# Two attention-fed feed-forward layers on one core: two border operands read out of PSUM, a slack in the planner, a shorter stretch of attention, and hidden values of the second part kept in PSUM

## The chip, the core and the metric

The kernel runs on one core of a Trainium2 chip, as one program. The metric is the device time of one execution in microseconds (us), lower is better. The core has a matrix engine (PE, with its weight loads PEld), a vector engine (DVE), a scalar engine (ACT), a second, general vector engine (POOL) and SP, which here only issues DMA transfers. Each works through its own instructions strictly in the order in which they were written; semaphores order them against each other. SBUF is the on-chip memory. PSUM is the small memory that PE writes to, here eight banks of 128 x 512 floats. GpSimd (POOL) is given no PSUM operand anywhere in this kernel.

## The reference

```python
def reference(q, k, v, w_gate, w_val, w_out1, w_in, w_out2):      # names shortened
    x = attention(q, k, v)                # 4 x 8 heads x 576 x 64, causal window of 128, ALiBi bias, softmax
    x = x.transpose(0, 2, 1, 3).reshape(2304, 512)
    g = x @ w_gate                        # 512 x 1536
    x = (g * sigmoid(g) * (x @ w_val)) @ w_out1       # 1536 x 512
    h = x @ w_in                          # 512 x 2048
    return (h * sigmoid(h)) @ w_out2      # 2048 x 512, all in float32
```

## The kernel before

The 2304 tokens are worked on in three **parts** of 768 (six tiles of 128). For each part come attention, the first feed-forward layer (`moe1`, six groups of 256 hidden columns) and the second (`moe2`, eight groups). The attention of a part is spread over the feed-forward work of the part before it, so that PE has something in all gaps. In the trace the second part's layers lie from about 375 to 680 us, with the third part's attention spread over them.

A float32 product is made of three passes of rounded pieces: each operand is split into `hi` (a rounded copy) and `lo` (the rest), so every operand costs a copy and a subtraction. The copy is `copy_op` (ACT, or DVE instead; line 348 or 349). The subtraction is `sum_op`: with `psum=True` always DVE (line 357), else POOL (line 358) or DVE, whichever the planner finds free earlier.

Each group's input products go by Strassen's scheme: `quad` runs seven products into three PSUM banks X, Y, Z with small sums in between. The second of them goes to bank Y; then DVE adds a saved product to Y in place (`add_to`, line 948), ACT copies Y out (`copy`, line 348), and only then may the fifth product overwrite Y. Between them PE has two other products (12 matmuls). `L963` is the last sum of `quad`, into a `tmp` buffer. The Strassen operands of the tokens are seven slots of the tile `XOP`. They are made at the **borders** between two layers by `operands`, out of `ACC` (the sums of `moe1`'s output) or `XST` (attention output, or `moe2`'s input side): some slots are split directly, the others are differences that `less` (line 693) writes into PSUM first. Slot 0 holds the first block (tokens 0 to 383 of the part) and feeds the first product of the next layer.

After `quad`, `hidden1` or `hidden2` apply the activation (`tanh`, line 1015, and `times`, line 1026). With `psum=False` the last `times` writes an SBUF buffer `tmp`, which frees the PSUM bank, and the split reads `tmp`. With `psum=True` it writes back into the PSUM bank, and the split into `h` reads the bank and frees it. One of the four blocks of a group has no bank, and goes by `tmp` in either case. Part one and the last groups of part three run with True, part two with False.

`out1` (lines 1182 to 1196) and `out2` (lines 1212 to 1227) multiply `h` by the output weights `wo` (three buffers) and add into `ACC`. In part two, `out_sums` also makes Strassen sums of output weights for part three: it fetches two halves of a weight (`word` and `top`, line 865), adds them, forms four `sums`, splits each into a `later_raw` buffer and stores that to DRAM (line 769).

The order on every engine comes from a **planner**: each operation is handed to `plan.add` with an estimated cost, a due time, what it reads and writes, and the banks it takes or gives. `issue` then plays a clock: per engine it takes the ready operation of the earliest due time and writes it down. An operation's estimated ready time is

```python
ready_at[m][o] = max(ready_at[m][o], end + handover(o, e))
```

where `handover` is what the planner counts from one engine's end to another's start, in ns (the first name is the one that waits):

```python
HANDOVER = {
    "pe": {"act": 370, "dve": 360, "pool": 300},
    "act": {"pe": 200, "dve": 128, "pool": 85},
    "dve": {"pe": 200, "act": 145, "pool": 85},
```

The clock is only an estimate. What it writes is the fixed order in which the engine will run, so an operation that is really later than planned holds up all that stands behind it.

Of the kernel before, what the change touches and what calls it, by code (L numbers as in the profile page):

```python
# [20 lines left out]
P = 128  # L21
# [35 lines left out]
class Plan:  # L57
# [18 lines left out]

    def add(self, engine, cost, due, fn, reads=(), writes=(), take=None, give=None, port=False, other=()):
        n = len(self.ops)
        preds = set()
        for key in reads:  # L80
            if key in self.writer:
                preds.add(self.writer[key])
            self.readers.setdefault(key, []).append(n)
        for key in writes:
            if key in self.writer:
                preds.add(self.writer[key])
            preds.update(self.readers.pop(key, ()))
            self.writer[key] = n
        preds.discard(n)
        if isinstance(take, Bank):  # L90
            take = (take,)
        ways = {e: (c, f, p or e == "pool", d) for e, c, f, p, d in [(engine, cost, fn, port, 0.0), *other]}
        self.ops.append((ways, due, preds, take, give))

    def issue(self):
# [25 lines left out]
        def start(e, n, now):  # L121
            ways, _, _, take, _ = ops[n]
            if ways[e][2]:
                now = max(now, port_free)
            if take is not None:
                m = len(take)
                if len(self.banks) < m or any(used[k] + m > self.limits[k] for k in kinds(take[0])):
                    return None
                now = max(now, heapq.nsmallest(m, self.banks)[-1][0])
            if len(ways) > 1 and min(ways, key=lambda o: done(o, n)) != e:  # L130
                return None
            return now
# [27 lines left out]
        while left:  # L160
# [5 lines left out]
            s, n = best  # L166
            ways, due, _, take, give = ops[n]
            cost, fn, port, _ = ways[e]
# [24 lines left out]
            for m in succs[n]:  # L193
                for o in ready_at[m]:
                    ready_at[m][o] = max(ready_at[m][o], end + handover(o, e))
                missing[m] -= 1
                if not missing[m]:
                    offer(m)
# [3 lines left out]
def attention_moe_moe2_kernel(  # L202
# [46 lines left out]
    GP = 3  # L249
# [96 lines left out]

    def copy_op(n, due, out, src, reads, writes, give=None, psum=True):
        act = lambda: nc.scalar.activation(out(), src(), AF.Copy)  # L348
        dve = lambda: nc.vector.tensor_copy(out(), src())
        plan.add(  # L350
            "act", cost("act_ps" if psum else "act", n), due, act, reads, writes, give=give,
            other=[("dve", cost("dve", n), dve, not psum, 500.0)],
        )

    def sum_op(n, due, out, x, y, op, reads, writes, give=None, psum=False):

# [4 lines left out]
        else:  # L361
            plan.add(
                "pool", cost("pool", n), due, pool, reads, writes, give=give,
                other=[("dve", cost("dve", n), dve, True, 500.0)],
            )
# [308 lines left out]
    def operands(src, name, due, plain=True):  # L674
# [5 lines left out]
        def block(j, blk, kk):  # L680
            c = 2 * j + kk
            return (
                lambda: src[:, blk * BT:blk * BT + BT, c, :],
# [18 lines left out]
        for kk in range(2):  # L702
            t1[kk] = less(b[0, 1, kk], b[0, 0, kk])
            t2[kk] = less(b[1, 1, kk], t1[kk])
# [56 lines left out]

    def split_weight(dst, key, src, reads, n, due, old=()):
        out = dst if callable(dst) else lambda: dst
        copy_op(n, due, lambda: out()[:, 0], lambda: src, reads, [key, *old], psum=False)
        sum_op(n, due, lambda: out()[:, 1], lambda: src, lambda: out()[:, 0].bitcast(F32), ALU.subtract, reads, [key])

# [20 lines left out]

    def strassen_sums(a, due):
        def add(x, y, op):
            i = take("sum", len(SUM_R))  # L790
            t, tk = SUM_R[i], ("sum", i)
            (xa, xk), (ya, yk) = x, y
            sum_op(2 * P, due, lambda: t, lambda: xa, lambda: ya, op, xk + yk, [tk])
            return t, [tk]
# [61 lines left out]
    def out_sums(kind, g, due, behind):  # L856

        a = {}
        for j in range(2):
# [9 lines left out]
            for i in range(2):  # L869
                a[i, j] = (w[:, 2 * P * i:2 * P * i + 2 * P], [wk])  # L870
        for n, (t, tk) in enumerate(strassen_sums(a, due)):
            m = take("stage", len(STAGE))
            u, uk = STAGE[m][0], ("stage", m)
            split_weight(u, uk, t, tk, 2 * P, due, before.pop(uk, ()))
            store(KEPT["s" + kind][g, n], lambda u=u: flat(u()), uk, ("kept", "s" + kind, g, n), due, 730.0)
# [289 lines left out]
    def value2(c, due):  # L1165
# [5 lines left out]
        return value  # L1171

    def out1(g, ws, d, blk, hs, due):
        b0, nb = blk
# [17 lines left out]
        keys = [("acc", b0 + t, d) for t in range(nb)]  # L1192
        if g == 0:
            copy_op(n, due, lambda: acc, pv, [b], keys, give=b)
# [34 lines left out]

    WLEAD = 19050.0  # L1230
    pend = []
    jobs = [("1", g) for g in range(G1 - 1)] + [("2", g) for g in range(G2 - 2)]
# [137 lines left out]
    operands(XST, "xt", state["t"])  # L1370
    spread(2, state["t"] + 6000.0, M1 + M2 - 8000.0)
    moe1(1, range(GP), "sum", False)
    moe1(1, range(GP, G1), "kept", False)
    flush()
    operands(ACC, "acc", state["t"])
    moe2(1, "kept", False)
    flush()
# [41 lines left out]
```

## Time and profile before

| | us |
|---|---|
| three timed executions | 935.42, 941.37, 941.68 (median 941.37) |
| the profiled execution | 937.67, of which the span from first to last instruction is 936.0 |
| PE busy in the span | 907.9 |
| DVE, POOL, ACT busy in the span | 708.9, 559.6, 531.0 |

A line such as `L948 DVE TENSOR_TENSOR bank<-bank,tmp` is one group of instructions: line of the kernel, engine, operation, what it writes and reads. "Idle before" is time that the engine stood still ahead of them and `<-` what ended it.

### The profile page before, as it was taken

Reading aid. Unit: us, or ns where it says so; the run is one execution under the profiler, and the core shown is the slowest. Engines: PE = TensorE matmul, PEld = TensorE weight load, DVE = VectorE, ACT = ScalarE, POOL = GpSimd, SP = SyncE. Lnnn points to the kernel's source line nnn. Section 1 sums busy time; section 2 is a strip of 40 time slices with the busy share of each in tenths; the row PEclk is TensorE's granted clock in tenths of the full one; section 3 lists DMA queues with packets and bytes.
Section 4 is the critical chain, followed back from the end, with each engine's and each line's share of the span. In section 5 each row is a group of like instructions: output and inputs, shape, how many; then the busy total and the mean of one; then the engine's idle time right before and its main releaser. Section 6 shows DMA issues by size and latency. Waiting matters only on the chain.

```text
span 936.0 us, 17803 instructions
## 1 busy us (share of the span) xinstructions
PE 907.9 (97%) x5758; PEld 843.8 (90%) x5758; DVE 708.9 (76%) x1602; ACT 531.0 (57%) x1361; POOL 559.6 (60%) x635
## 2 busy tenths in 40 slices
PE   7999999998999999999999999999999999999998
PEld 5799999997888888989999988888799999999996
DVE  7888879879889788647565867667755776778875
ACT  6887567757877675664343575445355333474431
POOL 2865468777657678785524487754144445876453
PEclk9999999999999999999999999999999999999999
DMA  9988997996897987999877789988498888678702
GB/s 222 281 243 258 283 324 221 294 313 206 274 304 260 305 290 265 354 314 304 279 219 244 242 292 330 312 284 311 151 329 249 251 253 253 201 234 245 218 23 91
DMA packets 181677, 241.58 MB, mean 258 GB/s; under 512 B 68048, under 2 KB 97232, under 8 KB 181584
## 3 DMA queue, kind: packets, MB, share of 16 engines
q1 hardware_dynamic: 181584, 240.44, 80.0%
q8 instruction: 46, 0.75, 0.3%
q14 instruction: 47, 0.39, 0.1%
HBM read 169.61 MB, written 70.78 MB: 257 GB/s over the span
## 4 chain that ended last, share of the span: by engine, by line
PE 69%; DVE 12%; DMA 7%; POOL 4%; ACT 4%; issue 3%; SPq 0%; DVEq 0%; POOLq 0%; ACTq 0%
PE bank L902 13%; PE bank L904 12%; PE bank L903 12%; PE bank L1212 4%; PE bank L1214 4%; PE bank L1213 4%; PE bank L607 3%; PE bank L493 3%; PE bank L1182 2%; PE bank L1184 2%; PE bank L1183 2%; DVE word L755 2%; DMA top<-kept_o 2%; PE bank L1118 1%; PE bank L1120 1%
## 5 line engine op out<-in xcount | busy, mean ns | idle before, releaser
L902 PE MATMUL bank<-XOP,wu 128*128 128x384 f32 (+1 forms) x868 | 297.3, 343 | 11.6 <-DVE tmp L963 4.3
L903 PE MATMUL bank<-XOP,wu 128*128 128x384 f32 (+1 forms) x868 | 288.9, 333 | 2.5 <-POOL XOP L358 1.9
L904 PE MATMUL bank<-XOP,wu 128*128 128x384 f32 (+1 forms) x868 | 288.9, 333 | 0.0
L902 PEld LDWEIGHTS bank<-XOP,wu 128*128 128x128 f32 x868 | 163.1, 188 | 23.0 <-ACT tmp L348 8.2
L903 PEld LDWEIGHTS bank<-XOP,wu 128*128 128x128 f32 x868 | 163.3, 188 | 4.4 <-POOL XOP L358 2.1
L904 PEld LDWEIGHTS bank<-XOP,wu 128*128 128x128 f32 x868 | 163.0, 188 | 0.1
L358 POOL TENSOR_TENSOR h<-tmp,h 128x384 fp32r<-128x384 f32 x77 | 81.7, 1071 | 62.0 <-ACT h L348 60.9
L348 ACT ACTIVATE tmp<-bank 128x384 f32<-128x384 f32 x133 | 62.1, 488 | 52.8 <-PE bank L904 28.2
L1026 DVE SCALAR_TENSOR_TENSOR tmp<-tmp,bank 128x384 f32<-128x384 f32 (+1 forms) x120 | 64.4, 542 | 36.4 <-ACT tmp L1015 24.4
L1212 PE MATMUL bank<-wo,h 128*128 128x512 f32 (+1 forms) x218 | 87.3, 401 | 1.7 <-DMA wo<-kept_o 1.7
L1214 PE MATMUL bank<-wo,h 128*128 128x512 f32 (+1 forms) x218 | 85.6, 393 | 0.0
L1213 PE MATMUL bank<-wo,h 128*128 128x512 f32 (+1 forms) x218 | 85.6, 393 | 0.0
L553 POOL TENSOR_TENSOR cs<-cs,st 128x512 f32<-128x512 f32 x36 | 39.9, 1109 | 65.8 <-DVE st L550 44.7
L1224 DVE TENSOR_TENSOR ACC<-bank,ACC 128x512 f32<-128x512 f32 (+1 forms) x97 | 64.1, 678 | 15.4 <-PE bank L1214 14.6
L358 POOL TENSOR_TENSOR wu<-word,wu 128x256 fp32r<-128x256 f32 x63 | 51.1, 824 | 39.4 <-ACT wu L348 35.2
L348 ACT ACTIVATE h<-tmp 128x384 fp32r<-128x384 f32 x97 | 49.5, 523 | 41.9 <-PE bank L1213 20.0
L1182 PE MATMUL bank<-h,wo 128*128 128x384 f32 (+1 forms) x216 | 72.5, 336 | 0.1
L1183 PE MATMUL bank<-h,wo 128*128 128x384 f32 (+1 forms) x216 | 71.5, 331 | 0.1
L1184 PE MATMUL bank<-h,wo 128*128 128x384 f32 (+1 forms) x216 | 71.4, 330 | 0.0
L1015 ACT ACTIVATE tmp<-bank 128x384 f32<-128x384 f32 (+1 forms) x121 | 57.0, 482 | 25.0 <-PE bank L904 11.5
L755 DVE SCALAR_TENSOR_TENSOR word<-raw,top 128x512 int32<-128x512 int32 x68 | 60.9, 895 | 11.7 <-ACT top L752 9.6
L948 DVE TENSOR_TENSOR bank<-bank,tmp 128x384 f32<-128x384 f32 x93 | 52.1, 561 | 22.1 <-PE bank L904 20.3
(414 smaller groups left out, 2149.6 us busy)
## 6 DMA issues: line engine op xcount, KB each, us to landing
wu<-kept_i SPq DMA_DIRECT2D x112, 256.0 KB, 3.5
wu<-kept_g SPq DMA_DIRECT2D x72, 256.0 KB, 4.2
wu<-kept_v SPq DMA_DIRECT2D x72, 256.0 KB, 4.3
wo<-kept_o SPq DMA_DIRECT2D x34, 512.0 KB, 4.7
raw<-in_moe_w_out_dram SPq DMA_DIRECT2D x28, 512.0 KB, 4.9
kept_o<-wo SPq DMA_DIRECT2D x28, 512.0 KB, 4.4
kept_i<-wu SPq DMA_DIRECT2D x56, 256.0 KB, 4.5
kept_s<-later_raw SPq DMA_DIRECT2D x44, 256.0 KB, 4.8
```

Of the source, the lines that this page charges most:

```text
L348: act = lambda: nc.scalar.activation(out(), src(), AF.Copy)
L358: pool = lambda: nc.gpsimd.tensor_tensor(out(), x(), y(), op)
L755: lambda: nc.vector.scalar_tensor_tensor(w.bitcast(I32), word, 13, top, ALU.logical_shift_right, ALU.bitwise_or),
L902: nc.tensor.matmul(ps, wh, xh, start=start, stop=False, skip_group_check=True)
L903: nc.tensor.matmul(ps, wh, xl, start=False, stop=False, skip_group_check=True)
L904: nc.tensor.matmul(ps, wl, xh, start=False, stop=stop, skip_group_check=True)
L1182: nc.tensor.matmul(ps[:, 0:n], wh, h[:, 0], start=(i == 0), stop=False)
L1183: nc.tensor.matmul(ps[:, 0:n], wh, h[:, 1], start=False, stop=False)
L1184: nc.tensor.matmul(ps[:, 0:n], wl, h[:, 0], start=False, stop=(i == 1))
L1212: nc.tensor.matmul(ps, hh, wh, start=(i == 0), stop=False)
L1213: nc.tensor.matmul(ps, hh, wl, start=False, stop=False)
L1214: nc.tensor.matmul(ps, hl, wh, start=False, stop=(i == 1))
```

## The change

1. `plan.add` gets a `slack`, which is added to the estimated ready time. `strassen_sums` and the splits inside `out_sums` get 4000 ns of it; the addition of the two fetched halves ahead of them doesn't.
2. At the border from `moe1` to `moe2`, in all three parts, the last group's sums for the first block's first two column blocks stay in PSUM: the sum is written over the bank, and `operands` makes slot 0 and the first difference from there.
3. The attention of the third part is spread over a stretch that is 20,000 planner ns shorter.
4. Part two runs `moe1` and `moe2` with `psum=True`.

```diff
-    def add(self, engine, cost, due, fn, reads=(), writes=(), take=None, give=None, port=False, other=()):
+    def add(self, engine, cost, due, fn, reads=(), writes=(), take=None, give=None, port=False, other=(), slack=0.0):
...
-                    ready_at[m][o] = max(ready_at[m][o], end + handover(o, e))
+                    ready_at[m][o] = max(ready_at[m][o], end + handover(o, e) + ops[m][5])
...
         def block(j, blk, kk):
             c = 2 * j + kk
+            if src is ACC and j == 0 and blk == 0:
+                return (lambda b=left[kk]: tiles(b.tile[:, 0:N])), [left[kk]]
...
-            t1[kk] = less(b[0, 1, kk], b[0, 0, kk])
+            held = src is ACC
+            t1[kk] = less(b[0, 1, kk], b[0, 0, kk], x_keys(0, kk) if held else (), left[kk] if held else None)
...
-        for n, (t, tk) in enumerate(strassen_sums(a, due)):
+        for n, (t, tk) in enumerate(strassen_sums(a, due, LATE)):
             m = take("stage", len(STAGE))
             u, uk = STAGE[m][0], ("stage", m)
-            split_weight(u, uk, t, tk, 2 * P, due, before.pop(uk, ()))
+            split_weight(u, uk, t, tk, 2 * P, due, before.pop(uk, ()), LATE)
...
-        if g == 0:
+        if g == G1 - 1 and b0 == 0 and d < 2:
+            plan.add("dve", cost("dve", n), due, lambda: nc.vector.tensor_tensor(pv(), pv(), acc, ALU.add), keys, [b])
+            left[d] = b
+        elif g == 0:
...
+    LATE = 4000.0
...
-    spread(2, state["t"] + 6000.0, M1 + M2 - 8000.0)
-    moe1(1, range(GP), "sum", False)
-    moe1(1, range(GP, G1), "kept", False)
+    spread(2, state["t"] + 6000.0, M1 + M2 - 28000.0)
+    moe1(1, range(GP), "sum", True)
+    moe1(1, range(GP, G1), "kept", True)
...
-    moe2(1, "kept", False)
+    moe2(1, "kept", True)
```

What it does to the order shows at three places. First DVE at the border from `moe1` to `moe2` of the first part (215 to 221 us of the trace before). `bank_132` and `bank_134` are the last output sums of the first block, lines 1196 and 693 of before are 1205 and 695 of after, and the sum that stays in PSUM is line 1200. Before:

```order
L1196 TENSOR_TENSOR ACC<-bank_132,ACC 128x3x128
L357 TENSOR_TENSOR XOP<-bank_129,XOP 128x384
L1196 TENSOR_TENSOR ACC<-bank_134,ACC 128x3x128
L1196 TENSOR_TENSOR ACC<-bank_135,ACC 128x3x128
L1196 TENSOR_TENSOR ACC<-bank_133,ACC 128x3x128
L693 TENSOR_TENSOR bank_130<-ACC 128x384
L693 TENSOR_TENSOR bank_132<-ACC,bank_130 128x384
```

After:

```order
L1200 TENSOR_TENSOR bank_132<-bank_132,ACC 128x384
L357 TENSOR_TENSOR XOP<-bank_129,XOP 128x384
L1200 TENSOR_TENSOR bank_134<-bank_134,ACC 128x384
L357 TENSOR_TENSOR XOP<-bank_132,XOP 128x384
L695 TENSOR_TENSOR bank_130<-ACC,bank_132 128x384
L357 TENSOR_TENSOR XOP<-bank_134,XOP 128x384
L695 TENSOR_TENSOR bank_132<-ACC,bank_130 128x384
L758 SCALAR_TENSOR_TENSOR word_98<-raw_94,top_95 128x512
L1205 TENSOR_TENSOR ACC<-bank_135,ACC 128x3x128
```

The two `lo` halves of slot 0 (`XOP<-bank_132`, `XOP<-bank_134`) now stand on DVE right behind the sums that they need; before, they stood on POOL, behind weights. A weight operation (`word_98`) has moved up into the border, ahead of the remaining sums.

Second, ACT in the third group of the second part (around 417 us before). `later_raw` are the splits of `out_sums`, `qts` and `KR` belong to attention, and line 1015 (1018 after) is the tanh. Before:

```order
L348 ACTIVATE KR<-bank_129 128x2x128
L348 ACTIVATE later_raw_256_4727<-sums 128x256
L1015 ACTIVATE tmp_108<-bank_134 128x384
L348 ACTIVATE later_raw_256_4727<-sums 128x256
L456 ACTIVATE qts<-bank_131 128x256
L348 ACTIVATE later_raw_256_4746<-sums 128x256
L1015 ACTIVATE tmp_110<-tmp_111 128x384
L348 ACTIVATE later_raw_256_4746<-sums 128x256
```

After:

```order
L348 ACTIVATE KR<-bank_132 128x2x128
L348 ACTIVATE tmp_109<-bank_129 128x384
L348 ACTIVATE tmp_110<-bank_128 128x384
L456 ACTIVATE qts<-bank_133 128x256
L1018 ACTIVATE tmp_108<-bank_130 128x384
L348 ACTIVATE later_raw_256_4773<-sums 128x256
L1018 ACTIVATE tmp_110<-tmp_111 128x384
L1018 ACTIVATE tmp_109<-bank_128 128x384
L1018 ACTIVATE tmp_111<-bank_129 128x384
L348 ACTIVATE later_raw_256_4825<-sums 128x256
```

The first split of `out_sums` has moved behind the first tanh and behind two copies of `quad`, and only two of the four stand in this stretch.

Third, SP at the end of the second part (around 665 us before). `wo_91<-kept_o_142` is the second half of the output weights of the last group, `kept_s` are the stores of `out_sums`, `later_l` are weights of the third part in buffers that attention used. Before:

```order
L772 DMA wu_79<-kept_g 128x512
L891 DMA later_l_256_7182<-kept_o_141 128x2x256
L891 DMA later_l_256_7185<-kept_o_141 128x2x256
L772 DMA wo_91<-kept_o_142 128x1024
L891 DMA later_u_256_7200<-kept_s_143 128x512
```

After:

```order
L775 DMA wu_79<-kept_g 128x512
L772 DMA kept_s_144<-later_raw_256_4825 128x512 x2
L775 DMA wo_91<-kept_o_142 128x1024
L775 DMA wo_92<-kept_o_141 128x1024
L772 DMA kept_s_144<-later_raw_256_4773 128x512
```

The fetch into `wo_91` no longer stands behind `later_l`, but behind two stores of `out_sums`, whose data POOL makes behind six operations on `XST` for the next border.

## Rows read from the trace of the kernel before

**Rows 1.** Page, busy time, share of the span and instructions of each engine.

```profile
PE   907.9 (97%) x5758; PEld 843.8 (90%) x5758; DVE 708.9 (76%) x1602; ACT 531.0 (57%) x1361; POOL 559.6 (60%) x635
```

**Rows 2.** Page, the chain that ended last, by engine.

```profile
PE 69%; DVE 12%; DMA 7%; POOL 4%; ACT 4%; issue 3%; SPq 0%; DVEq 0%; POOLq 0%; ACTq 0%
```

**Rows 3.** Waits of PE, 200 to 240 us: total us, times, longest us.

```profile
PE bank L903 <- POOL XOP L358: 1.9, 1, 1.9
PE bank L902 <- ACT tmp L348: 1.9, 2, 1.1
PE bank L902 <- DVE tmp L349: 0.7, 1, 0.7
```

**Rows 4.** Waits of PE, 240 to 375 us.

```profile
PE bank L902 <- DVE tmp L963: 1.9, 3, 1.2
PE bank L902 <- DVE tmp L349: 1.0, 1, 1.0
```

**Rows 5.** Waits of PE, 375 to 680 us.

```profile
PE bank L902 <- DVE tmp L963: 2.4, 3, 1.9
PE bank L902 <- ACT tmp L348: 2.2, 4, 0.8
PE bank L1212 <- DMA wo<-kept_o: 1.7, 1, 1.7
PE bank L903 <- DVE XOP L357: 0.2, 1, 0.2
```

**Rows 6.** Waits of PE, 680 to 936 us.

```profile
PE bank L1120 <- DVE later_cs L357: 0.6, 1, 0.6
PE bank L902 <- DVE bank L693: 0.3, 1, 0.3
```

**Rows 7.** Windows: us, busy us of PE, PEld, DVE, ACT, POOL; clock, DMA.

```profile
240.00:375.00 135.00, 132.04 (x762) 114.05 (x761) 117.28 (x247) 95.78 (x244) 93.53 (x112) 1.00 0.84 282
375.00:680.00 305.00, 298.35 (x1833) 275.11 (x1832) 205.17 (x466) 155.24 (x405) 175.61 (x207) 1.00 0.84 280
```

**Rows 8.** Timeline of PE, 203 to 232 us: start, us, what, idle before.

```profile
220.16 0.45 PE L903 MATMUL bank<-XOP,wu 128*128 128x384 f32 x1 [1.87 <-POOL XOP L358]
...
229.11 0.34 PE L903 MATMUL bank<-XOP,wu 128*128 128x384 f32 x1
229.28 0.34 PE L904 MATMUL bank<-XOP,wu 128*128 128x384 f32 x1
```

**Rows 9.** Timeline of POOL, 203 to 232 us.

```profile
216.53 1.31 POOL L358 TENSOR_TENSOR wo<-word,wo 128x512 fp32r<-128x512 f32 x1
217.80 6.52 POOL L358 TENSOR_TENSOR XOP<-ACC,XOP 128x384 fp32r<-128x384 f32 x6
```

**Rows 10.** Timeline of ACT, 414 to 420 us.

```profile
417.60 0.42 ACT L348 ACTIVATE later_raw<-sums 128x256 fp32r<-128x256 f32 x1 [2.11 <-POOL sums L358]
417.92 0.47 ACT L1015 ACTIVATE tmp<-bank 128x384 f32<-128x384 f32 x1
```

**Rows 11.** Timeline of POOL, 404 to 422 us.

```profile
415.46 1.30 POOL L358 TENSOR_TENSOR word<-word,top 128x512 f32<-128x512 f32 x1 [2.05 <-DMA word<-kept_o]
```

**Rows 12.** Groups of instructions by form, 375 to 680 us.

```profile
L358 POOL TENSOR_TENSOR h<-tmp,h 128x384 fp32r<-128x384 f32 x39 | 40.8, 1057 | 28.4 <-ACT h L348 28.4
L348 ACT ACTIVATE tmp<-bank 128x384 f32<-128x384 f32 x58 | 27.1, 488 | 22.6 <-PE bank L904 11.3 <-DVE bank L948 11.0
L948 DVE TENSOR_TENSOR bank<-bank,tmp 128x384 f32<-128x384 f32 x40 | 22.3, 561 | 11.3 <-PE bank L904 10.3 <-ACT tmp L348 0.8
L348 ACT ACTIVATE later_raw<-sums 128x256 fp32r<-128x256 f32 x44 | 18.0, 414 | 30.7 <-POOL sums L358 26.0 <-DMA kept_s<-later_raw 4.2 <-ACT tmp L348 0.5
L357 DVE TENSOR_TENSOR h<-tmp,h 128x384 fp32r<-128x384 f32 x17 | 11.6, 697 | 2.3 <-ACT h L348 1.9
```

**Rows 13.** Groups of instructions by form, whole span.

```profile
L357 DVE TENSOR_TENSOR h<-bank,h 128x384 fp32r<-128x384 f32 x50 | 27.5, 550 | 5.3 <-ACT h L348 4.6
```

**Rows 14.** Timeline of SP, 640 to 684 us.

```profile
665.52 0.33 SPq L772 DMA_DIRECT2D wo<-kept_o  x1
```

More of the change, by code (lines that the diff above doesn't have):

```diff
@@ L92, in add @@
         ways = {e: (c, f, p or e == "pool", d) for e, c, f, p, d in [(engine, cost, fn, port, 0.0), *other]}
-        self.ops.append((ways, due, preds, take, give))
+        self.ops.append((ways, due, preds, take, give, slack))
     def issue(self):
@@ L121, in start @@
         def start(e, n, now):
-            ways, _, _, take, _ = ops[n]
+            ways, _, _, take, _, _ = ops[n]
             if ways[e][2]:
@@ L166, in issue @@
             s, n = best
-            ways, due, _, take, give = ops[n]
+            ways, due, _, take, give, _ = ops[n]
             cost, fn, port, _ = ways[e]
@@ L345, in cost, with copy_op @@
         return a + b * n
-    def copy_op(n, due, out, src, reads, writes, give=None, psum=True):
+    def copy_op(n, due, out, src, reads, writes, give=None, psum=True, slack=0.0):
         act = lambda: nc.scalar.activation(out(), src(), AF.Copy)
@@ L351, in copy_op, with sum_op @@
             "act", cost("act_ps" if psum else "act", n), due, act, reads, writes, give=give,
-            other=[("dve", cost("dve", n), dve, not psum, 500.0)],
+            other=[("dve", cost("dve", n), dve, not psum, 500.0)], slack=slack,
         )
-    def sum_op(n, due, out, x, y, op, reads, writes, give=None, psum=False):
+    def sum_op(n, due, out, x, y, op, reads, writes, give=None, psum=False, slack=0.0):
         dve = lambda: nc.vector.tensor_tensor(out(), x(), y(), op)
@@ L363, in sum_op @@
                 "pool", cost("pool", n), due, pool, reads, writes, give=give,
-                other=[("dve", cost("dve", n), dve, True, 500.0)],
+                other=[("dve", cost("dve", n), dve, True, 500.0)], slack=slack,
             )
@@ L760, in raw_weight, with split_weight @@
         return w, wk
-    def split_weight(dst, key, src, reads, n, due, old=()):
+    def split_weight(dst, key, src, reads, n, due, old=(), slack=0.0):
         out = dst if callable(dst) else lambda: dst
-        copy_op(n, due, lambda: out()[:, 0], lambda: src, reads, [key, *old], psum=False)
-        sum_op(n, due, lambda: out()[:, 1], lambda: src, lambda: out()[:, 0].bitcast(F32), ALU.subtract, reads, [key])
+        copy_op(n, due, lambda: out()[:, 0], lambda: src, reads, [key, *old], psum=False, slack=slack)
+        sum_op(n, due, lambda: out()[:, 1], lambda: src, lambda: out()[:, 0].bitcast(F32), ALU.subtract, reads, [key], slack=slack)
     def store(where, src, key, dkey, due, c):
@@ L786, in attention_moe_moe2_kernel, with strassen_sums @@
     ORDER_OUT = ("A11", "S1", "S3", "S4", "S2", "A12", "A22")
-    def strassen_sums(a, due):
+    def strassen_sums(a, due, slack=0.0):
         def add(x, y, op):
@@ L792, in add @@
             (xa, xk), (ya, yk) = x, y
-            sum_op(2 * P, due, lambda: t, lambda: xa, lambda: ya, op, xk + yk, [tk])
+            sum_op(2 * P, due, lambda: t, lambda: xa, lambda: ya, op, xk + yk, [tk], slack=slack)
             return t, [tk]
```

1 line of the change is left out of this document (added).

## The prediction

> **What bounds the kernel now.** I read the page's busy times first: PE is at work for 97% of the span [rows 1], and the chain that ended last is PE for 69% of it [rows 2]. The change neither adds nor removes a matmul (both orders have the same rows on PE), so it can only give back time in which PE waits, or make new waits. The second view is therefore the waits of PE, stage by stage. From 200 us on, where the order first differs a little later, they are 4.5 us up to 240 [rows 3], 2.9 up to 375 [rows 4], 6.5 up to 680 [rows 5] and 0.9 after that [rows 6]: 14.8 us, or 1.6% of the span. That is the ceiling of any gain. Last come the other engines: in the second part DVE is busy for 205.2 of 305 us (67%) and POOL for 175.6 (58%) [rows 7]. Neither is the bound, but each works in a fixed order, so a late instruction holds up what PE needs. Most of the waits (all those with L349, L963 or tmp L348) are of one kind: PE wants to overwrite a bank in `quad` and DVE or ACT hasn't read it out yet.
>
> **The border operand.** At the first border PE waits 1.87 us for POOL [rows 8]: the `lo` halves of slot 0 stand on POOL behind a weight split (216.53) and then come as six in a row in 6.52 us, or 1.09 each [rows 9]. Afterwards they are DVE operations on a PSUM bank, for which `h<-bank`, the same operation on as many elements, gives 0.55 us [rows 13], and stand right behind their sums. That removes this wait but for a remainder: ACT's copy and DVE's 0.55 still follow the last sum, so I leave 0.3 and take 1.6 back. The border's other waits (0.7 for L349, and 0.8, which is rows 3's 1.9 for ACT less its longest, 1.1, that lies ahead of the first difference in the order) come from DVE and ACT being full. DVE gets two more `lo` here (1.1 us), and a weight operation has moved into the border, while the differences lose an SBUF read. Bounds: they vanish (gain 1.5) or double (loss 1.5); I take a gain of 0.4, as POOL work leaves the border and the weight sums start sooner. Together 2.0 of 3.4. The borders of the second and third part have 0.2 [rows 5] and 0.3 [rows 6] that name the operands; counted at nothing.
>
> **The slack.** ACT stood idle for 30.7 us in front of the 44 `later_raw` copies, 26.0 of them for POOL's sums [rows 12]. Most of it hid no work for PE. The one great wait, 1.9 of the 2.4 us in rows 5, comes from there: the fetched half was late, so POOL began its addition only at 415.46 [rows 11], ACT waited 2.11 us for the sums at its first `later_raw`, and the tanh behind it started at 417.92 [rows 10]. With the slack that tanh stands ahead of the split. The addition of the halves has no slack, so POOL, and at times DVE, can still stand in front of a late transfer.
>
> **Values kept in PSUM.** Each of the 14 groups of the second part has four blocks, three with a bank. So 42 `lo` subtractions become DVE operations on PSUM at 0.55 us, 23.1 us in all. Before, the 56 were 39 on POOL at 1057 ns and 17 on DVE at 697 ns [rows 12]; the new order leaves 10 on POOL and 4 on DVE. DVE gains 23.1 - 13 x 0.697 = 14.0 us, POOL loses 29 x 1.057 = 30.7 us. DVE goes from 67% to about 72% of the stage, POOL from 58% to 48%. ACT's copy and the `times` stay. The row says that a subtraction out of PSUM is 0.15 us cheaper on DVE than one with both inputs in SBUF (550 against 697 ns). [...]
>
> What counts is whether the new DVE work stands ahead of `add_to`. Between the product that fills Y and the one that overwrites it PE has 12 matmuls, at 0.17 us from one start to the next [rows 8] 2.1 us; DVE's sum and ACT's copy take 0.56 + 0.49 = 1.05 [rows 12], and for the three hand-overs (PE to DVE, DVE to ACT, ACT to PE) the kernel's planner counts 0.20, 0.13 and 0.37. That leaves about 0.4 us. Of the program's 108 `add_to`, 13 stood in the order before directly behind a `lo` of `h` and 5 behind an addition that waits for a fetched weight half; afterwards 23 and 1. So short predictable work replaces long unpredictable work. The nearest row for such a stage is the first part's (240 to 375 us), where eight groups already run in this way with DVE at 87%: 2.9 us of waits [rows 4, 7], 0.36 a group. The second part had 4.6 us of this kind in 14 groups [rows 5], 0.33 a group, 1.9 of it the case above. Bounds for afterwards: nothing, or 14 x 0.36 = 5.1. DVE at 72% lies nearer the stage with 67% than the one with 87%; without the one great wait that stage has 2.7, and I take 2.5. The slack and the PSUM values together then give 4.6 - 2.5 = 2.1.
>
> **The shorter attention.** The last weighted sum of attention moves ahead by one group on PE, with one output product's worth of work after it before and a whole group after it now. The rate of attention per us of feed-forward goes up by some 8%; its DVE and ACT work fills the idle part of 33% and 49% [rows 7]. One would think that it also removes the 1.7 us wait for `wo` [rows 5], as the two `later_l` fetches, which wait for attention, leave the place ahead of it. But the fetch was issued at 665.52 [rows 14], when PE had only just done with that buffer, and PE has the same six products to do meanwhile in either order. I count nothing there. The cost to watch: the fetch now stands behind two stores whose data POOL makes after six operations on `XST`. In the order of PE the last two slots become free some 8 us of matmuls ahead of the buffer, and POOL then has two operations at 1.09 [rows 9], a sum and two splits to do, an estimate of 5 us. It should be in time with 3 us to spare; what POOL is later than that, PE waits more.
>
> **The sum.** 2.0 + 2.1 = 4.1 us; rounded to 4. The profiled execution of 937.67 would become 933.7. The median of the three timed runs is 941.37, 3.7 above that; the middle of the four executions lies between 937.67 and 941.37, at 939.5. I set the sum against that: 935.5, so **936 us**. About 1% (9.4 us) is what a measurement of this kernel can tell from no change, as its own runs lie 6.3 us apart.
>
> **The rivals.**
> (a) *The waits only move.* ACT and DVE stop waiting for `out_sums`, but the halves come late all the same; POOL stands still in front of them, and the border's `XOP` work behind it on POOL is late instead. For it: the slack isn't on the addition that waits, and DMA is busy for 84% of the stage [rows 7]. Then the gain is between -1 and 1 us: 939.5.
> (b) *Everything goes that the change touches*: the 3.4 us of the first border, and all 6.5 of the second part. For it: each wait has its cause in an edit. Against it: `wo` is not touched, and the first part kept 2.9. Time 939.5 - 9.9 = 929.6, say 930.
> (c) *DVE becomes late for `add_to`.* Place: `add_to` of each of the 14 groups. If two `lo` (1.1 us) stand ahead of it and DVE isn't ahead, they use up the margin of 0.4 and PE loses 0.7 in each group, 10 us: 949. It decides when DVE is more than 0.4 us behind as Y is full. Against it: DVE is idle for a third of the time, and the first part lost only 0.36 a group at 87%.
> (d) *Banks run out.* A bank is now held for the copy and the `lo` as well, 0.49 + 0.55 and a handover, 1.2 us. If PE had to wait that long once a group, it would be 14 x 1.2 = 17 us: 956. In the first part, which already holds its banks so, no wait of PE names `h` [rows 4]. [...]
>
> **Chances.** The forecast 0.55, (a) 0.20, (b) 0.12, (c) 0.10, (d) 0.03. The range of 930 to 945 us takes in the forecast, (a) and the upper half of (b), and leaves out (d), (c) mostly, and some of (b): about 0.2. Faster by over 1% (under 932.0) are most of (b) and the forecast's tail, 0.16; slower by over 1% (over 950.8) are (d) and a part of (c), 0.06; the rest 0.78.
>
> **What the profile after would show.** The border: no wait of PE for POOL's `XOP` near 220 us. The slack: ACT's idle time ahead of `later_raw` clearly under 30.7 us, and no wait of 1.9 near 419. PSUM: `h<-bank` on DVE x92 at about 0.55, POOL's `h<-tmp` x48, and waits of PE for L963, L349 and tmp L348 in the second part of 2 to 3 us. Attention: the wait for `wo` near the end of the second part still there. I am wrong if the second part's waits rise above 6.5 us, by L948's chain for (c) or a bank of `h` for (d), if the wait for `wo` grows by several us behind the stores, or if the waits are as forecast and the time isn't.

## The result, and the profile after

The changed kernel takes 927.83 us (four executions, 926.28 to 931.11) against 940.45 beside it: a ratio of 0.9878, interval 0.9849 to 0.9908. A second measurement gave 928.47 (six) against 938.43: 0.9894, 0.9866 to 0.9921. So it is faster by 10 to 12.6 us, and the prediction of 936 with a range from 930 is wrong: the change brings about three times the 4 us of its sum. The profiled execution took 931.11, its span is 929.4.

The page, busy times and the chain that ended last:

```profile
PE 909.7 (98%) x5758; PEld 845.7 (91%) x5758; DVE 703.4 (76%) x1623; ACT 529.8 (57%) x1362; POOL 529.0 (57%) x613
...
PE 74%; DVE 8%; POOL 6%; DMA 6%; issue 3%; ACT 2%; SPq 0%; POOLq 0%; DVEq 0%; ACTq 0%
```

PE is now 74% of the chain, 69% before [rows 2], and POOL works 31 us less [rows 1]. The waits of PE from 200 us on (us in total, times, longest):

```profile
PE bank L905 <- ACT tmp L348: 1.5, 4, 0.6
PE bank L905 <- DVE bank L695: 1.3, 1, 1.3
PE bank L1189 <- POOL h L358: 0.6, 1, 0.6
PE bank L1121 <- DVE tmp L1029: 0.6, 1, 0.6
PE bank L906 <- DVE XOP L357: 0.6, 2, 0.4
PE bank L905 <- DVE vld L966: 0.5, 1, 0.5
PE bank L607 <- POOL u L584: 0.5, 1, 0.5
PE bank L905 <- ACT XOP L348: 0.3, 1, 0.3
PE bank L905 <- DVE tmp L349: 0.2, 1, 0.2
```

That is 6.1 us where [rows 3 to 6] have 14.8. The wait for POOL at the border (1.9), the great one near 419 (1.9) and the one for `wo` (1.7) are gone; the longest left is 1.3. The groups by form, 375 to 680 us, show two of the edits at work, the PSUM values and the slack:

```profile
L357 DVE TENSOR_TENSOR h<-bank,h 128x384 fp32r<-128x384 f32 x42 | 22.7, 551 | 1.3 <-ACT h L348 0.7
...
L348 ACT ACTIVATE later_raw<-sums 128x256 fp32r<-128x256 f32 x44 | 18.0, 411 | 2.1 <-DMA kept_s<-later_raw 2.1
...
L358 POOL TENSOR_TENSOR h<-tmp,h 128x384 fp32r<-128x384 f32 x10 | 10.5, 1046 | 30.2 <-ACT h L348 30.2
...
L357 DVE TENSOR_TENSOR h<-tmp,h 128x384 fp32r<-128x384 f32 x4 | 2.5, 633 | 0.5 <-ACT h L348 0.3
```

ACT's idle time ahead of `later_raw` fell from 30.7 us [rows 12] to 2.1, and the `lo` halves stand where they were foretold: 42 on DVE out of PSUM, 10 on POOL, 4 on DVE out of SBUF. The PSUM form is the cheaper one again, 551 against 633 ns.

One thing in this profile is not a wait. The windows around two waits in the first part (us; busy us of PE, PEld, DVE, ACT, POOL; granted clock; DMA):

```profile
15.00:20.50 5.50, 3.73 (x30) 2.70 (x28) 4.74 (x27) 4.94 (x20) 2.20 (x3) 1.00 1.08 245
20.50:23.90 3.40, 3.40 (x22) 2.41 (x24) 2.09 (x5) 2.98 (x12) 3.33 (x5) 0.53 0.73 222
...
109.00:112.70 3.70, 2.12 (x12) 1.57 (x12) 2.65 (x5) 2.32 (x5) 1.42 (x2) 1.00 0.66 210
112.70:116.10 3.40, 3.40 (x13) 3.20 (x13) 2.60 (x5) 2.64 (x8) 2.25 (x3) 0.52 0.94 313
```

Right behind a wait of 1.7 and one of 1.4 us PE is busy all the time, but at half clock (from 112.91 us on 0.32 us from the start of one 128x384 product to the next, 0.17 at full clock): the trace's clock records give two stretches of 3.41 us at 0.5. Each costs half its length, 1.7 us, and lowers the mean granted clock by 0.0018; so the loss of any run can be read off its clock, as (1 - clock) x span. Ten runs of the change average 0.9986, a loss of 1.3 us; 35 runs of the kernel before average 0.9961, a loss of 3.6. The profile of before happened to have no such stretch, in spite of its four waits of 1.7 to 1.9 us, so it showed nothing of this term. The change's runs with a clock of 1.000 take 926.3 to 928.1 us, those with 0.996 take 931.1. At a clock of 1.000 nine runs of the kernel before average 936.1 us and five of the change 927.1: 9.0 us of the gain are there without the clock.

### The profile page after: what moved, and what is told of

Same layout as the page of the kernel before. It is cut to its first block, busy times and chain, and to the rows that moved or that the text cites. A ratio compares the mean times of both kernels' runs of the same rounds, so it can differ in the third digit from the quotient of the medians.

```text
span 929.4 us, 17799 instructions
## 1 busy us (share of the span) xinstructions
PE 909.7 (98%) x5758; PEld 845.7 (91%) x5758; DVE 703.4 (76%) x1623; ACT 529.8 (57%) x1362; POOL 529.0 (57%) x613
## 4 chain that ended last, share of the span: by engine, by line
PE 74%; DVE 8%; POOL 6%; DMA 6%; issue 3%; ACT 2%; SPq 0%; POOLq 0%; DVEq 0%; ACTq 0%
PE bank L905 14%; PE bank L906 13%; PE bank L907 13%; PE bank L1221 5%; PE bank L1222 5%; PE bank L1223 5%; PE bank L493 3%; PE bank L607 3%; PE bank L1189 2%; PE bank L1188 2%; PE bank L1190 2%; PE bank L570 2%; POOL h L358 1%; PE bank L1121 1%; PE bank L1122 1%
## 5 line engine op out<-in xcount | busy, mean ns | idle before, releaser
L905 PE MATMUL bank<-XOP,wu 128*128 128x384 f32 (+1 forms) x868 | 297.3, 343 | 4.7 <-ACT tmp L348 1.5
L905 PEld LDWEIGHTS bank<-XOP,wu 128*128 128x128 f32 x868 | 163.5, 188 | 14.4 <-ACT tmp L348 3.8
L358 POOL TENSOR_TENSOR h<-tmp,h 128x384 fp32r<-128x384 f32 x48 | 50.6, 1063 | 65.4 <-ACT h L348 64.3
L1029 DVE SCALAR_TENSOR_TENSOR bank<-tmp,bank 128x384 f32<-128x384 f32 (+1 forms) x98 | 52.7, 549 | 21.1 <-ACT tmp L1018 12.0
L348 ACT ACTIVATE h<-bank 128x384 fp32r<-128x384 f32 (+1 forms) x95 | 45.8, 484 | 39.2 <-DVE bank L1029 23.9
L758 DVE SCALAR_TENSOR_TENSOR word<-raw,top 128x512 int32<-128x512 int32 x68 | 57.8, 849 | 11.1 <-ACT top L755 10.0
```

What stands on the lines that cost most here:

```text
L358: pool = lambda: nc.gpsimd.tensor_tensor(out(), x(), y(), op)
L905: nc.tensor.matmul(ps, wh, xh, start=start, stop=False, skip_group_check=True)
```

## The experiments

**Theory 1**: the gain is the sum of PE's waits that each edit removes, plus the half-clock stretches that those waits bring. Rivals: **theory 2**, one edit carries it all; **theory 3**, any reshuffle of the planner's order does as much. The edits were switched by themselves:

```diff
-            if src is ACC and j == 0 and blk == 0:
+            if False and src is ACC and j == 0 and blk == 0:
...
-    LATE = 4000.0
+    LATE = 0.0
...
-    spread(2, state["t"] + 6000.0, M1 + M2 - 28000.0)
-    moe1(1, range(GP), "sum", True)
+    spread(2, state["t"] + 6000.0, M1 + M2 - 8000.0)
+    moe1(1, range(GP), "sum", False)
```

The first switch (with two more such lines, `held` and `left`) is the border, then the slack, the attention, the PSUM values (three calls). `only_x` has three of them thrown, `no_x` one. All results in one table: ratio to the kernel before, measured beside it; the mean granted clock of the timed runs; and from each one's profile the sum of the view of PE's waits by stretch.

| kernel | ratio [interval] | us | clock | 200-240 | 240-375 | 375-680 | whole span |
|---|---|---|---|---|---|---|---|
| before | 1 | 939.07 | 0.9961 | 4.5 | 2.9 | 6.5 | 23.1 |
| the change | 0.9878 [0.9849, 0.9908] | 927.83 | 0.9985 | 1.9 | 0.2 | 2.3 | 15.1 |
| after_again | 0.9894 [0.9866, 0.9921] | 928.47 | 0.9987 | 1.3 | 0.6 | 2.0 | 15.1 |
| only_border | 0.9954 [0.9931, 0.9978] | 935.67 | 0.9976 | 2.2 | 1.4 | 6.3 | 20.5 |
| only_slack | 0.9986 [0.996, 1.0011] | 937.11 | 0.9976 | 3.6 | 1.6 | 7.1 | 21.7 |
| only_spread | 1.0001 [0.998, 1.0022] | 939.26 | 0.9968 | 3.3 | 1.8 | 6.3 | 20.4 |
| only_psum | 0.9969 [0.9946, 0.9991] | 936.29 | 0.9978 | 3.3 | 1.6 | 4.9 | 19.1 |
| no_border | 0.9924 [0.9902, 0.9947] | 932.87 | 0.9970 | 3.3 | 1.7 | 2.6 | 17.6 |
| no_slack | 0.9942 [0.9918, 0.9966] | 935.37 | 0.9979 | 2.2 | 1.4 | 7.1 | 22.2 |
| no_spread | 0.9969 [0.9952, 0.9986] | 937.01 | 0.9951 | 2.7 | 1.2 | 7.0 | 21.5 |
| no_psum | 0.9908 [0.9885, 0.9931] | 930.88 | 0.9980 | 1.9 | 1.7 | 2.1 | 16.1 |
| no_spread_local | 0.9993 [0.9975, 1.001] | 938.47 | 0.9952 | 2.3 | 0.5 | 7.5 | 20.9 |
| no_spread_b1 | 0.9946 [0.9923, 0.9969] | 934.28 | 0.9965 | 1.7 | 0.8 | 5.0 | 18.1 |
| no_spread_b2 | 0.9955 [0.9931, 0.9979] | 934.48 | 0.9958 | 1.7 | 1.4 | 6.7 | 20.7 |
| slack_psum | 0.9901 [0.9877, 0.9925] | 930.00 | 0.9985 | 3.5 | 1.7 | 2.0 | 16.5 |
| spread24 | 0.9897 [0.9876, 0.9918] | 929.26 | 0.9987 | 1.9 | 2.6 | 4.6 | 18.8 |
| border_once | 0.9879 [0.9846, 0.9912] | 927.95 | 0.9993 | 1.5 | 2.5 | 1.4 | 16.2 |
| border_once28 | 0.9905 [0.9876, 0.9934] | 930.87 | 0.9983 | 1.7 | 1.0 | 3.0 | 16.1 |

The waits are those of one execution each, and identical orders show how far one can be trusted. Ahead of 200 us all these kernels run the same order, and their waits there come to between 8.0 and 9.9 us. From 200 to 375 us `only_slack`, `only_spread`, `only_psum`, `no_border` and `slack_psum` run the order of before: 4.9 to 5.2 us, where before's own profile has 7.4. That profile was an unlucky one.

**Each edit alone.**

> The kernel before with the border operand in PSUM alone. Theory 1 (the gain is the sum of PE's waits that each edit removes): 0.3% to 0.6% faster, 3 to 5 us, from the 200 to 240 us stretch and, as the profile after suggests, from 240 to 375 us too, where PE's waits fell from 2.9 to 0.2 us. Theory 2 (one edit carries it): over 0.9% faster. Theory 3 (any new order from the planner moves the time as much): any value within 1%, and the waits of 375 to 680 us change as much as those before.

> The kernel before with the slack of 4000 alone. Theory 1: 0.2% to 0.4% faster, 2 to 4 us; the wait of 1.9 us near 419 us is gone and ACT's idle time ahead of the later_raw copies falls from 30.7 us to under 20; the stretch before 375 us stays as it was. Theory 2: over 0.9% faster if this is the one edit. Theory 3: any value within 1%.

> The kernel before with the shorter stretch of attention alone. Theory 1, as predicted: no change (within 0.2%), the 1.7 us wait for wo stays. Theory 1 as the profile after corrects it: 0.2% faster, as that wait goes when attention no longer stands between the outputs of the last groups. Theory 2: over 0.9% faster. Theory 3: any value within 1%.

> The kernel before with the second part's hidden values kept in PSUM alone. Theory 1: within 0.3%; short splits on DVE replace POOL's, the waits of 375 to 680 us fall by 1 to 2 us, and the one near 419 us (out_sums) stays. Rival (c) of the prediction: slower by up to 1% with waits on L963 and tmp L348 in most groups. Theory 2: over 0.9% faster. Theory 3: any value within 1%.

Alone they give 0.46, 0.14, 0 and 0.31%, 0.9% together against 1.1 to 1.2 for the whole: no edit carries it, and the reshuffled orders of the slack and of the attention gave nothing clear of noise. The border's 0.46%, 4.3 us (interval 2.1 to 6.5), is more than its profile shows: it has as many waits as the attention's, 20.5 and 20.4. The attention's kernel lost the wait for `wo`, as the corrected theory 1 has it, but was no faster: 6.3 us of other waits stand in its second part. The slack took away all of ACT's idle time ahead of `later_raw` (30.7 to 0.0) and yet left 7.1 us of waits in the second part, now spread over seven causes. In the border kernel the great wait stayed, and this execution shows what else it can cost:

```profile
413.00:416.50 3.50, 3.50 (x24) 3.43 (x23) 1.46 (x3) 1.15 (x3) 1.05 (x2) 1.00 1.05 397
416.50:419.50 3.00, 0.90 (x6) 0.62 (x5) 0.95 (x3) 1.77 (x5) 2.84 (x5) 1.00 1.07 382
419.50:422.90 3.40, 3.28 (x11) 3.18 (x12) 2.05 (x6) 1.98 (x6) 3.40 (x6) 0.54 1.02 368
```

PE idles for 2.2 us (0.90 busy of 3.00) and then works at 0.54: 11 matmuls where the window ahead has 24.

**The change less one edit.**

> The change without its border operand (slack, PSUM values and shorter attention stay). Theory 1 (each edit removes its own waits of TensorE; alone the border gave 4.3 us, the slack 1.3, the PSUM values 2.9, the attention 0; the missing 2.7 of 11.2 come from edits together): the wait of 1.9 us for GpSimd near 220 us is back, and the time is 932, 4 above the whole change, with a granted clock under that of the whole change since a half-clock stretch can follow that wait. Theory 2 (one edit carries it, and it is the border): 936 or more. Theory 3 (any reshuffle of the order gives as much): 928, as the order is another one again.

> The change without the slack. Theory 1: 929.5, 1 to 2 above the whole change; ScalarE's idle time ahead of later_raw back at about 30 us, with at most one wait of TensorE of about 2 us from it. Theory 2 (the slack carries it in company of the others): 936. Theory 3: 928.

> The change with the long stretch of attention of the kernel before. Theory 1: 928 to 929, and the wait for wo at the end of the second part is back (1.7), which would be the 1 us. Theory 2 (the attention carries it in company of the others): 936. Theory 3: 928, whatever the waits are.

> The change with the second part's values split out of SBUF as before. Theory 1: 931, 3 above the whole change, with waits of TensorE in the second part of 4 to 5 us instead of 2.3. Theory 2 (the PSUM values carry it): 936. Theory 3: 928.

Border and PSUM values came out as theory 1 has it, at 932.9 and 930.9, though `no_psum` not by the waits expected: 2.1 us in the second part, not 4 to 5. By the ratios (the change: 0.9886, the mean of its two) the slack is worth 5 us in company, where it gave 1.3 alone, and the attention, worth nothing alone, 8: simple addition fails. The profile without the attention's edit shows one wait that no other kernel so far had:

```profile
PE bank L905 <- ACT XOP L348: 4.5, 2, 4.1
PE bank L1221 <- DMA wo<-kept_o: 1.1, 1, 1.1
```

**Is it a late transfer?** At that border, near 530 us, POOL stood 5.6 us for a fetched weight half, with `lo` halves of operands behind it: rival (a) of the prediction. This kernel leaves those transfers out:

```diff
+        at_border = kind == "1" and g == 4
...
-                    "sp", 730.0, due + 1800.0 * j, lambda src=src, dst=dst: nc.sync.dma_start(out=dst, in_=src),
+                    "sp", 730.0, due + 1800.0 * j, lambda src=src, dst=dst: None if at_border else nc.sync.dma_start(out=dst, in_=src),
```

> The change without the shorter attention (937.0 in the run before), and without the four transfers that bring the weight halves of the one group whose additions stand on GpSimd among the operands' lo halves of the border near 530 us; what is added there is old data, so that group's products in the third part are wrong. The order is otherwise the same. In the trace with them GpSimd stood 5.6 us for that transfer, and TensorE waited 4.1 for the operands behind it. Theory A (a late transfer in front of the border is what this kernel loses by): the wait of 4.1 goes to under 1, and the time from 937 to 931 or 932, as the clock is also less often halved. Theory B (GpSimd and ScalarE are too full at that border in this order, whatever the transfer does): 3 us or more of the wait stay, and the time is 936 to 937.

The wait stayed at 4.1 and the time at 938: theory A falls. The chain of that kernel's trace (start us, us, what) shows what it was:

```profile
529.57 0.50 ACT tmp L1019
530.09 0.57 DVE bank L1030
530.69 0.50 ACT h L348
531.28 0.57 DVE h L357
531.87 0.57 DVE bank L695
532.47 0.57 DVE bank L695
533.07 0.50 ACT XOP L348
533.61 0.69 PE bank L906
```

The difference for the border's operands (L695) stands on DVE behind the activation and the `lo` half of a block of the very group that it feeds. The order without the attention's edit, with the banks' numbers, says why:

```
L1029 SCALAR_TENSOR_TENSOR bank4_132<-tmp6_112,bank4_132 128x384
L357 TENSOR_TENSOR h4_104<-bank4_132,h4_104 128x384
L695 TENSOR_TENSOR bank4_132<-ACC_65,bank5_133 128x384
L695 TENSOR_TENSOR bank5_133<-ACC_65,bank4_132 128x384
```

The difference takes bank 4, and that block frees it: the planner had no other bank for it. Of the eight, bank 5 is the border's `left[1]`, one holds an earlier difference, three hold this group's own products, two the first products of the next group, and one belongs to attention. This is rival (d). Three kernels test it, all with the long stretch of attention: PSUM values undone for one group (`b1`: the last of `moe1`; `b2`: the first of `moe2`), or the border operand left out (`slack_psum`).

```diff
-    moe1(1, range(GP, G1), "kept", True)
+    moe1(1, range(GP, G1 - 1), "kept", True)
+    moe1(1, range(G1 - 1, G1), "kept", False)
```
```diff
-                hs[i, b] = hidden2(c[i, b], N, psum, t0 + 7.0 * pe_cost(6, N))
+                hs[i, b] = hidden2(c[i, b], N, psum and (part == 0 or g > 0), t0 + 7.0 * pe_cost(6, N))
```

> The change without the shorter attention, and with the values of one group (the last of the gated layer in the second part) split out of SBUF as before. In the order without it, the three differences for the second half of a border's operands near 530 us find no free PSUM bank but the one of the X product of the very group they feed: they stand on VectorE behind that block's lo half. Here they stand ahead of it. Bank theory: the wait of 4.1 us goes to under 0.7, and with it the half-clock stretch behind it (1.7): 937 less 6, 931. If it is only ScalarE and VectorE that are full there: the wait stays at 3 or more, 936 to 937.

> The change without the shorter attention, with the values of one group (the first of the second layer in the second part) split out of SBUF as before. The differences still take the bank of that group's X block, but right behind the operation that reads it out, no longer behind ScalarE's copy (0.50), VectorE's lo half (0.57) and two hand-overs. Bank theory: the wait shrinks from 4.1 by 1.2 to 2.9 and doesn't go; 935 to 936. If not the bank but the load of the engines: 4.1 as before, 937.

> Slack and PSUM values alone, without border operand and shorter attention. Without the border operand no bank is held from the last output product to the differences. Bank theory: no wait of 4.1 near 530; what stays are the border's wait for GpSimd near 220 (1.9) and the one for wo near 671 (1.1 to 1.8): 933 to 934. If the PSUM values alone use up the banks: the wait of 4.1 is there, 938. If each edit gives the same alone as with others, 939 - 1.3 - 2.9 = 935.

In `b1` no wait for ACT's `XOP` on L905 is left. In `b2` it shrank by what ACT's copy (0.50 in the chain above), DVE's `lo` (0.57) and the hand-overs last, from 4.1 to 2.9 as expected:

```profile
PE bank L905 <- ACT XOP L348: 3.3, 2, 2.9
PE bank L905 <- ACT tmp L348: 1.9, 2, 1.5
PE bank L1221 <- DMA wo<-kept_o: 1.5, 1, 1.5
```

Their times, 934.3 and 934.5, are less sharp than their waits: `b1` has other waits in that stage, 5.0 us, where 931 needed fewer. `slack_psum` has no such wait either and is at 930.0, by the ratios 6 us ahead of the kernel that adds the border operand to it. That is also 3 to 4 us under what was expected; the wait for `wo` is gone there too. So slack and PSUM values alone bring 0.99% where the whole change brings 1.14%. The last two leave the operand out at the later borders alone, with the long and the short attention:

```diff
-        if g == G1 - 1 and b0 == 0 and d < 2:
+        if g == G1 - 1 and b0 == 0 and d < 2 and not state.get("part"):
...
+    left.clear()
+    state["part"] = 1
     moe2(0, "raw", True)
```

> Slack, PSUM values and the border operand at the first border alone (near 220 us), attention's stretch as in the kernel before. At the border near 530 no bank is held for the operand. Bank theory: no wait of 4.1 us there, and against slack and PSUM values alone (930.0) the wait for GpSimd near 220 goes from 1.9 to about 1.3 for VectorE: 928 to 930, 7 to 9 under the change without the shorter attention, from which it differs only in the border operand of the second and third part. If that one's loss had to do with something else than the banks held: 935 or more.

> The same with the shorter attention of the change. By the sum of waits it is the change itself, as its second and third border never waited for GpSimd: 927 to 930. Under 926 would say that the border operand cost something at the later borders of the whole change too.

`border_once` has the whole gain (927.95) without the attention's edit, and 1.4 us of waits in the second part in place of 7.0. So the loss of 8 us without that edit came from the operand held at the later borders. With the shorter attention the order at that border finds its banks; `border_once28`, at 930.87 a little over what was expected, lies inside the change's interval, so the change itself loses nothing there that can be told from noise. Neither the operand at the later borders nor the shorter attention is needed for the gain.

**One order among many?**

> The whole change with attention's stretch shortened by 24 in place of 28 us (before: 8). The same edits, but another order from about 375 us on. If the edits carry the gain: 928 to 930, with TensorE's waits from 200 us on at 6 to 8 us. If the gain is an accident of one order: anywhere between 928 and 937, with a new single wait of over 2 us that can be named.

929.3 with another order from 407 us on, no wait over 1.3: the gain isn't one order's accident. But its waits from 200 us on are 10.8 us, not 6 to 8, so the sum of one profile's waits gives the time only roughly.

**What a wait costs.** Two kernels make PE wait on purpose, with the same sum in long and in short pieces. In some groups ACT's copy of bank Y is repeated:

```diff
+        def act():
+            for _ in range(1 + again):
+                nc.scalar.activation(out(), src(), AF.Copy)
...
-        u2 = copy("Y")
+        n = take("quad", 1000)
+        u2 = copy("Y", 5 if n % 7 == 3 else 0)
```

(short: `2 if n % 2 == 1`).

> The whole change once more, beside the kernels below. [...] Expected: 927 to 930, and by the theory that half-clock stretches make the scatter, runs with a granted clock of 1.000 about 3 us shorter than those with 0.996.

> The whole change, with ScalarE's copy of u2 made six times in place of once in 7 of the groups, all over the kernel; no other instruction is added or moved. TensorE's product into Y behind it should wait for 5 x 0.49 less the margin of 0.4, 2.05 us, in each: 14 us of waits. If a wait costs what it lasts: 928 + 14 = 942 at a granted clock as that of the whole change (0.998). If a long wait also brings a stretch of 3.41 us at half clock, as behind the waits of 1.4 to 2.2 us in the runs so far, each costs 1.7 more: 942 + 7 x 1.7 = 954 where all do, and a granted clock of 0.985.

> As the kernel with the long waits, but with the copy made three times in 26 of the groups: 52 extra copies in place of 35, each wait of TensorE 2 x 0.49 - 0.4 = 0.58 us, 15 us in all. If a wait costs what it lasts: 928 + 15 = 943, as in the kernel with the long ones. If only long waits bring half-clock stretches: also 943, at a granted clock as that of the whole change, and so 10 or more below the kernel with the long ones. If it is the sum of the waits that counts for the clock: both far above 943.

Long: 947.99 us at a mean clock of 0.9930. Short: 943.45 at 0.9974. Of the seven waits made so in the long kernel, one brought a half-clock stretch in this profile:

```profile
712.00:716.00 4.00, 4.00 (x25) 4.00 (x24) 3.48 (x7) 2.32 (x6) 1.81 (x2) 1.00 0.75 255
716.00:720.10 4.10, 1.78 (x10) 1.46 (x9) 0.00 (x0) 3.50 (x8) 4.10 (x5) 1.00 0.64 204
720.10:723.50 3.40, 3.40 (x13) 3.38 (x12) 1.23 (x3) 1.31 (x3) 2.15 (x3) 0.52 0.30 77
723.50:728.00 4.50, 4.50 (x27) 4.50 (x27) 3.67 (x8) 0.87 (x2) 0.11 (x1) 0.98 0.63 169
```

Summing over PE's matmuls the time from one start to the next above the median of that shape, less 1.7 for each half-clock stretch, the waits grew by 14.2 us (long) and 12.8 (short). The clock's loss grew by 0.0057 x 943 = 5.4 and 0.0013 x 940 = 1.2. The sums, 19.6 and 14.0, meet the measured 19.5 and 15.0. So by this count waits of nearly the same sum cost 4.5 us more in long pieces. The count matters: by the view of PE's waits, which lists few of the short ones, the sums grew by 12.6 and 8.2 and differ by 4.4 themselves. The clock's part doesn't hang on it. The clock takes 5.4 us with the seven long ones, 0.8 for each: less than the 1.7 expected, since only some of them bring a stretch.

## Why the prediction was wrong, by its steps

*The ceiling* ("14.8 us [...] the ceiling of any gain"). PE alone bounds the kernel, and the gain lies in its waits: that held in the main. But a wait's own length is not all that it costs. The waits in the whole span fell by 8.0 us and the clock's loss by 2.3, together 10.3 of the 10 to 12.6 measured. In all 18 rows of the table, median less waits less clock loss lies between 909 and 916 us, while the medians go from 928 to 939. The clock is not in my sum, and accounts for 2.3 of the missing 6 to 8.5 us; the waits were the larger miss, 8.0 against 4.1. The two parts don't weigh the same as evidence. That the clock has only some 2 us of it is seen without a profile, as 9.0 us are left at a clock of 1.000. The 8.0 sets before's unlucky execution against two of the change; with the 4.9 to 5.2 us of the other kernels from 200 to 375 us it would be under 6. So by estimate some 3 us of the gain stand in no wait that the view lists, and no run here places them.

*The border* (2.0 forecast). The stretch 200 to 240 fell from 4.5 to 1.9 and 1.3. But the five other kernels with before's order have 3.3 to 3.6 there, and the twelve profiles with the change's order 1.3 to 2.7, 1.9 in the mean. So the waits fell by about 1.5: the mechanism is right, and by the waits the size a little high. The remainder is not 0.3 behind ACT's copy but 1.3 for a difference on DVE (L695). Without this edit POOL's 1.9 is back in `no_border`, and the time is by the ratios 3 to 4 us higher.

*The slack and the PSUM values* (4.6 to 2.5, a gain of 2.1). The mechanism is right, and this term was too small. Of the waits it spoke of (for `tmp` from ACT or DVE, lines 348, 349 and 966, which was 963) 1.1 and 0.8 us are left between 375 and 680 in the change's two profiles, a gain of 3.5 to 3.8. Alone the two edits leave 7.1 and 4.9 us of all waits in that stage, together 2.0 (`slack_psum`). In `no_psum` border, slack and attention reach 2.1 as well, so other relief can stand in for the PSUM values; the slack can't be spared (`no_slack`, 7.1). Why the slack needs a partner, these runs show only by the waits, not by a cause. Not in the sum: small waits for other operands grew, by about 1.0 us in that stage and 0.8 after it.

*`wo`* ("I count nothing there"). This step failed: 1.7 us went. The lead was judged rightly: without the wait the product that needs the fetch would come 4.2 us after its issue before (671.42 less 1.73 less 665.52), and it comes 4.0 after it now. What it took for fixed is the transfer, 5.8 us before and 3.2 after. Before, two `later_l` fetches stand right in front of it in the queue; in the change none does:

```profile
663.80 1.39 SPq L891 DMA_DIRECT2D later_l<-kept_o  x2
665.52 0.33 SPq L772 DMA_DIRECT2D wo<-kept_o  x1
671.42 0.47 PE L1212 MATMUL bank<-wo,h 128*128 128x512 f32 x1 [1.73 <-DMA wo<-kept_o]
...
657.14 0.85 SPq L772 DMA_DIRECT2D kept_s<-later_raw  x2
661.14 1.02 SPq L775 DMA_DIRECT2D wo<-kept_o  x2
665.15 0.39 PE L1221 MATMUL bank<-wo,h 128*128 128x512 f32 x1
```

The two landed only 1.4 and 3.3 us after the `wo` fetch was issued. The 18 profiles of the table divide by this. In the eight in which `later_l` stands in front (before, `only_border`, `only_slack`, `only_psum`, and the long stretch with the operand at every border) the transfer took 4.8 to 5.9 us and PE waited 0.7 to 1.8 for it. In the other ten it took 3.2 to 3.7 without a wait, but for `no_slack` with 4.6 and 0.6. In `only_border`, `only_psum` and `no_spread_b1` the view names ACT for this wait, yet PE starts 0.13 us after the landing, as in before (0.14). `only_spread`, which differs from before by attention's stretch alone, has 3.2 us; `slack_psum` and `border_once` have the long stretch, but `later_l` behind the fetch. So the thought that the prediction set aside, that it helps when the two fetches "leave the place ahead of it", was the right one. No run moves these fetches by themselves.

*The stretch 240 to 375*, counted at nothing, went from 2.9 to 0.2 and 0.6. Most of that is chance in one execution: the five kernels that run before's order there have 1.6 to 1.8, and the twelve profiles with the change's order 0.2 to 2.6, 1.3 in the mean.

*The attention* (0). Right alone, at 1.0001, though by waits that came in place of the one for `wo`. In company it decides whether the later border finds its banks, which I had not seen.

*The rivals.* (a) fell with the waits: they went, and did not move. (b), 930 at 0.12, came nearest, in part by luck: of its 9.9 us of waits 6.8 to 7.7 went by before's one profile, and the clock, which it didn't count, made up the rest. (c) didn't occur. (d), put at 0.03 on the ground that the first part holds its banks without a wait [rows 4], doesn't occur in the change, but is real: 4.1 us in one place as soon as three holders of banks meet. Rows 4 alone could not show it. *The median* on which the sum was set, 939.5, was right: 938.4 to 940.5 in six measurements.

So three steps failed: the price of a wait, which left out the clock (2.3 us); `wo`, put at nothing on its lead alone, while its transfer became 2.5 us shorter (1.7 us of waits); and the size of the term for slack and PSUM values (2.1 forecast, 3.5 to 3.8 measured).

## What to carry to other kernels

Price a wait of PE by its length and by what the clock does behind it (here 0.8 us more for each of the seven long ones), and look for that in the granted clock of several runs, not in one profile. Before adding up edits of an order, list the buffers that each of them holds longer (here PSUM banks), and look where all of them meet: an edit that is worth nothing alone may be what keeps two others apart. A wait that names ACT or a copy may be the last link of a chain that began with a bank: follow the chain back until an operation stands behind the consumer of its own result. For a fetch that comes late, look at what stands in front of it in the queue (here two fetches, 5.8 us against 3.2) as well as at when it is issued.

## What was not expected of the hardware

PE's clock fell to half (0.5) for 3.41 us, twice in the change's profile: 0.25 us behind the end of a wait of 1.72 and 1.39 behind one of 1.44. It fell again 2.5 us after the program's last product. In `hold_long` it fell about 0.9 us behind a wait of 2.32, and in `only_border` in the window behind one of 2.2. In `no_spread_local` the first product behind the wait of 4.1 already took 0.69 us, where 0.44 followed the wait in `hold_long`. Not every such wait brings it: in the long-wait kernel's profile one of the seven did, and before's profile had none behind waits of 1.7 to 1.9 us. Identical executions differ by 4 to 6 us along with it (the kernel before: 936 at a clock of 1.000, 942 at 0.995).

The same `wo` transfer took 4.8 to 5.9 us with two fetches in flight in front of it (5.8 in before's profile), and 3.2 to 3.7, once 4.6, without (3.2 in the change's).
